# Unread mask matmuls, another split of normalisation and copies, and a third probability buffer in the first attention batch

## The chip, the cores and the metric

The kernel runs on one core of a Trainium2 chip. The metric is the device time of one execution in microseconds (us). TensorE does matrix products, VectorE (DVE) and ScalarE (ACT) elementwise work and reductions, GpSimd (POOL) elementwise work between SBUF tiles, and SyncE (SP) issues almost all DMAs.

## The reference

Attention over 8 batches, 8 heads, 576 tokens, 64 features, followed by a two-layer feed-forward network over all 4608 tokens. Heads 0 to 3 have a plain causal window of 32, heads 4 to 7 a dilated one.

```python
scores = scale * np.matmul(q, k.transpose(0, 1, 3, 2))          # scale = 1/8
mask_plain = (rel >= 0) & (rel < 32)
mask_dil = (rel >= 0) & (rel < 128) & (rel % 4 == 0)
scores = np.where(mask, scores, -1e9); scores -= scores.max(-1)
attn = np.exp(scores); attn /= attn.sum(-1) + 1e-09
x = (attn @ v) with heads side by side                           # 4608 x 512
h = x @ w_in; g = where(h > 0, h, exp(min(h, 0)) - 1)            # 4608 x 2048
out = g @ w_out                                                  # 4608 x 512
```

The weights arrive in a 64-bit format. The kernel converts them to float32 on chip, with one scaling on ScalarE (`magnitude`) and three integer operations on VectorE (`convert`).

## The kernel before, in words

Only the blocks inside the window are computed. Heads go in pairs (`hp` 0 to 3), so one batch has four pairs. A pair has 6 query blocks of 96 rows per head, each against short key pieces, so that its probabilities are 96 partitions by 12 by 64 numbers (`sm`).

The change touches the first batch alone (`first_attention`, generators advanced by a list of steps written out by hand). Every instruction of these steps is kept in program order on its engine. For a pair the steps of before are:

- **S**: two mask matmuls set the score bank to 0 or -1e9, then 72 small score matmuls add the scores (banks `a` and `b`, by turns).
- **M**: VectorE takes the maximum (`nmx`, L356) and subtracts it (L359), ScalarE takes the exponential (L361). For pairs 1 to 3 a tiny GpSimd copy (L119) makes the next weight loads wait for the maximum.
- **P**: VectorE sums (L363), adds 1e-9 (L326) and takes the reciprocal (L327). The multiplication (L328) is VectorE's for pairs 0 and 3, GpSimd's for 1 and 2.
- **T** and **U**: TensorE transposes the probabilities against an identity into a bank (`c` or `a`), and eight copies of the two heads bring them into one of two zeroed buffers `pt` (L381 on VectorE, L383 on ScalarE). T has the transposes and the first head's copies, U the second head's.
- **O**: 12 products of `pt` and values into bank `d` or `b`, then ScalarE copies them into `x` (L314, L317).

Letters A to D are weight conversion (A: ScalarE's scaling; B, C, D: the three VectorE operations on the first tile, the second, and the other two). G0, G1 and G2 are single matmuls of the network's first product, `h<-x,a`, one for each pair's slice of `x`. After the list the code emits the network's first 512 tokens: conversion, `h` products, ELU and second products `o_ps`, with batch 1's attention between them; from there on a scheduler sets the order on each engine by estimated times. Everything later, up to the end at 870.7 us, is a long stream of such products on TensorE.

Buffers: probabilities of pairs 1 to 3, and the inputs of pairs 2 and 3, lie in ring slots that weights will use later.

Of the kernel before, what the change touches and what calls it, by code (L numbers as in the profile page):

```python
# [10 lines left out]
F32 = mybir.dt.float32  # L11
# [5 lines left out]
ALU = mybir.AluOpType  # L17
# [4 lines left out]
DM, DFF = H * D, 2048  # L22
NT = B * S
P = 128
# [50 lines left out]
def body(ctx: ExitStack, tc: tile.TileContext, q, k, v, masks, w_in, w_out, out):  # L75
# [18 lines left out]

    early2 = [wst.tile([P, 2, 4 * DM], F32, name=f"r{NR - NE + i}") for i in range(NE)]
    early = [early2[i // 2][:, i % 2, :] for i in range(2 * NE)]
    for z in pt:
        nc.gpsimd.memset(z, 0.0)

    raw2, raw, full4, full2, full = [None] * (NF // 2), [None] * NF, [None] * (NF // 2), [None] * NF, [None] * 2 * NF  # L100
# [217 lines left out]
                                           in_=flat.rearrange("p (s c i) -> p s c i", c=DIL, i=G // DIL)))  # L318
        return last

    def outputs(b, hp, places, vt, tr, keep=lambda ins: ins):
        products(places, vt, tr)
        return copies(b, hp, places, keep)

    def normalise(eng, sm, sums, keep):
        keep(nc.vector.tensor_scalar(out=sums, in0=sums, scalar1=1e-9, scalar2=None, op0=ALU.add))  # L326
        keep(nc.vector.reciprocal(out=sums, in_=sums))  # L327
        return keep(eng.tensor_tensor(out=sm, in0=sm, in1=sums.unsqueeze(2).broadcast_to([QB, 2 * NU, 2 * G]), op=ALU.mult))  # L328

    def transposed():  # L330
        count[0] += 1
        return pt[count[0] % len(pt)]
# [5 lines left out]
    def first_attention(hp, loaded):  # L338

        dil = hp >= NPAIR // 2  # L340
        qt, kt, vt = loaded
        if hp > 0:
            room, o = (early[0], WINDOW + 2 * S) if hp == 1 else (early[2 * (hp - 2) + 1], 2 * NU * D)
            sm = room[:QB, o:o + 2 * NU * 2 * G].rearrange("p (u j) -> p u j", u=2 * NU)
        else:
            sm = ap.tile([QB, 2 * NU, 2 * G], F32, name="sm", bufs=1)
        mx = ap.tile([QB, 2 * NU], F32, name="nmx", bufs=4)
        sums = ap.tile([QB, 2 * NU], F32, name="sums", bufs=4)
        s_ps = ps_f.tile([P, 2, TC], F32, name="ab"[hp % 2])[:QB, :, :NU * 2 * G]
        for h in range(2):  # L350
            mm(s_ps[:, h, :], ones_sb, mask_sb[:, int(dil), :], start=True, stop=False)
        scores([s_ps[:, h, :] for h in range(2)], qt, kt, False)
        yield
        s4 = s_ps.rearrange("p h (n j) -> p h n j", n=NU)
        mx4 = mx.rearrange("p (h n) -> p h n", h=2)
        inorder(nc.vector.tensor_reduce(out=mx4, in_=s4, op=ALU.max, axis=mybir.AxisListType.X))  # L356
        if hp > 0:
            load_w(hp, mx)
        inorder(nc.vector.tensor_tensor(out=sm.rearrange("p (h n) j -> p h n j", h=2), in0=s4,  # L359
                                        in1=mx4.unsqueeze(3).broadcast_to([QB, 2, NU, 2 * G]), op=ALU.subtract))  # L360
        inorder(nc.scalar.activation(out=sm, in_=sm, func=AF.Exp, scale=0.125))  # L361
        yield
        inorder(nc.vector.tensor_reduce(out=sums, in_=sm, op=ALU.add, axis=mybir.AxisListType.X))  # L363
        last = normalise(nc.vector if hp in (0, NPAIR - 1) else nc.gpsimd, sm, sums, inorder)
        if hp == NPAIR - 1:
            last_step[hp] = last.ins
        yield
        tr = transposed()

        t_ps = (ps_c, ps_f)[hp % 2].tile([P, 2, TC], F32, name="ca"[hp % 2])  # L370
        for n in range(NU):
            for h in range(2):
                o = n % NA * QB
                mm(t_ps[h * 2 * G:(h + 1) * 2 * G, n // NA, o:o + QB], sm[:, h * NU + n, :], ident, start=True, stop=True)
        t4 = t_ps[:, :, :NA * QB].rearrange("p i (n q) -> p i n q", n=NA)
        for h in range(2):
            to = tr[:, h * NU:(h + 1) * NU, :].rearrange("p (i n) q -> p i n q", i=2)
            for c, r, m in ((0, 0, 2), (1, 0, 1), (1, 1, 1), (2, 0, 2)):
                cs, ks, rs = slice(c * G, (c + 1) * G), slice((c + r) * G, (c + r + m) * G), slice((h * 2 + r) * G, (h * 2 + r + m) * G)
                if hp == NPAIR - 1 or (hp, h) == (1, 0):  # L380
                    inorder(nc.vector.tensor_copy(out=to[ks, :, :, cs], in_=t4[rs, :, :, cs]))  # L381
                else:
                    inorder(nc.scalar.copy(out=to[ks, :, :, cs], in_=t4[rs, :, :, cs]))  # L383
            yield
        a_ps = ps_f.tile([P, 2, TC], F32, name="db"[hp % 2])
        yield outputs(0, hp, [(a_ps[:, i, :], i * NA, (i + 1) * NA) for i in range(NU // NA)], vt, tr, inorder)

    def exponential(u, sm, nmx, sums):
        nc.scalar.activation(out=sm[:, u, :], in_=sm[:, u, :], func=AF.Exp, bias=nmx[:, u:u + 1], scale=0.125, accum_out=sums[:, u:u + 1])  # L389
# [558 lines left out]
    its = [first_attention(hp, rooms[hp]) for hp in range(NPAIR)]  # L948


    for what in "S0 S1 M0 M1 S2 P0 M2 T0 U0 S3 P1 P2 A0 M3 T1 U1 O0 T2 U2 P3 B0 O1 T3 U3 O2 G0 G1 O3 G2 A1 C0 D1".split():
        i = int(what[1])
        if what == "G0":
            ps_second.close()
# [2 lines left out]
        if what[0] == "A":  # L957
            inorder(magnitude(i))
        elif what[0] in "BCD":
            last_conversion = convert(i // 2, inorder, {"B": slice(0, DM), "C": slice(DM, 2 * DM), "D": slice(2 * DM, 4 * DM)}[what[0]])  # L960
        elif what[0] == "G":
            next(first)
        else:
            last_copy = next(its[i])
    ready = 2
# [173 lines left out]
```

## Time and profile before

| what | value |
|---|---|
| three runs, median | 873.62 us (872.38 to 873.66) |
| profiled execution: its time, its span | 872.5 us, 870.7 us |
| TensorE busy | 853.7 us (98%) |
| VectorE, ScalarE busy | 555.7 us (64%), 526.9 us (61%) |
| GpSimd busy | 75.0 us (9%) |
| first network product `h<-x,a` starts | 28.02 us |
| granted TensorE clock, mean | 0.996 |

The span runs from the first to the last instruction; 1.8 us of the execution lie outside it. A timeline row gives start, duration from the first start to the last end, engine, line, operation, output and inputs, and a count; in brackets stands how long the engine was idle before, and who ended that. The records of TensorE count two passes for each float32 product, so 12 products appear as x24, and the recorded matmul durations overlap: what one costs in a stream is the distance between starts.

### The profile page before, as it was taken

What the parts mean: (1) busy time and instruction counts of PE and PEld (TensorE: products, weight loads), DVE (VectorE), ACT (ScalarE), POOL (GpSimd) and SP (SyncE); (2) the same over time, 40 slices, a digit from 0 to 9 for tenths busy, and PEclk for the clock granted to TensorE, in tenths of its full rate; (3) what the DMA queues carried; (4) which work ended last, traced back from release to release, by engine and by line L of the source; (5) the groups of instructions that cost most, each with busy time, mean ns of one, the idle gap of its engine ahead of it and who ended that gap; (6) DMA issues with size and microseconds to landing.
All of it is one profiled execution on the core that took longest, in us unless ns stands there. A gap on an engine that the chain in (4) does not pass through costs nothing.

```text
span 870.7 us, 17559 instructions
## 1 busy us (share of the span) xinstructions
PE 853.7 (98%) x6788; PEld 722.5 (83%) x6788; DVE 555.7 (64%) x902; ACT 526.9 (61%) x1031; POOL 75.0 (9%) x112
## 2 busy tenths in 40 slices
PE   6999999999999999999999999999999999999998
PEld 4556878888878889888878898988899988999986
DVE  6899987766685857787765577545476635344431
ACT  3767987756585756667654575654566654555541
POOL 2013311000020200111010020100011100000000
PEclk8999999999999999999999999999999999999999
DMA  9997335134546346867753867662875652776441
GB/s 343 378 381 264 132 123 188 34 132 133 176 160 200 102 151 215 262 221 239 231 173 100 279 200 242 212 184 83 265 226 175 206 164 80 241 209 191 143 153 56
DMA packets 93459, 166.48 MB, mean 191 GB/s; under 512 B 9696, under 2 KB 40768, under 8 KB 93376
## 3 DMA queue, kind: packets, MB, share of 16 engines
q1 hardware_dynamic: 89200, 158.01, 57.0%
q10 hardware_dynamic: 4176, 7.34, 2.3%
q8 instruction: 54, 0.88, 0.4%
q14 instruction: 29, 0.24, 0.1%
HBM read 124.42 MB, written 40.89 MB: 190 GB/s over the span
## 4 chain that ended last, share of the span: by engine, by line
PE 84%; DVE 7%; ACT 4%; DMA 2%; issue 2%; POOL 1%; SPq 0%; ACTq 0%; DVEq 0%; POOLq 0%
PE o_ps L111 41%; PE h L111 34%; PE a_ps L111 8%; DVE a L152 1%; DMA out<-e 1%; POOL pt L435 1%; DVE a L154 1%; DMA r<-combined 1%; DVE nmx L410 1%; ACT sm L389 0%; ACT pt L383 0%; DVE sm L397 0%; PE a L111 0%; DMA kt<-k 0%; DVE a L144 0%
## 5 line engine op out<-in xcount | busy, mean ns | idle before, releaser
L111 PE MATMUL h<-xall,r 128*128 128x384 f32 (+1 forms) x708 | 156.9, 363 | 0.4 <-DVE e L634 0.2
L111 PEld LDWEIGHTS h<-xall,r 128*128 128x128 f32 x708 | 127.7, 188 | 17.2 <-issue 0.8
L111 PE MATMUL o_ps<-a,gh 128*128 128x512 f32 x394 | 129.0, 416 | 0.0
L448 DVE SCALAR_TENSOR_TENSOR a-1_3369<-a-1_3369,a 128x768 f32<-128x768 f32 x64 | 61.0, 953 | 87.9 <-ACT a L448 87.9
L111 PE MATMUL h<-r,r 128*128 128x384 f32 x476 | 108.3, 337 | 0.4 <-DMA r<-combined 0.4
L448 ACT COPY e<-h 128x384 f32<-128x384 f32 x96 | 46.0, 479 | 98.5 <-PE h L111 96.6
L111 PEld LDWEIGHTS o_ps<-a,gh 128*128 128x128 f32 x394 | 73.4, 188 | 21.8 <-issue 9.1
L448 ACT ACTIVATE a<-a-1_3369 128x384 f32<-128x384 f32 (+1 forms) x96 | 60.8, 634 | 50.0 <-DVE a-1_3369 L448 44.0
L111 PEld LDWEIGHTS h<-r,r 128*128 128x128 f32 x476 | 84.4, 188 | 4.0 <-ACT e L448 0.7
L111 PE MATMUL o_ps<-r,gh 128*128 128x512 f32 x242 | 75.4, 393 | 0.0
L111 PE MATMUL o_ps<-a,r 128*128 128x512 f32 x288 | 72.3, 392 | 0.0
L111 PE MATMUL o_ps<-a,gl 128*128 128x512 f32 x173 | 67.7, 391 | 0.0
L448 ACT ACTIVATE a<-a 128x768 f32<-128x768 f32 (+1 forms) x72 | 60.8, 845 | 1.9
L111 PEld LDWEIGHTS o_ps<-a,r 128*128 128x128 f32 x288 | 53.7, 188 | 9.9
L111 PE MATMUL h<-a,r 128*128 128x384 f32 x256 | 60.1, 336 | 0.0
L448 DVE TENSOR_TENSOR a-1_3369<-h,e 128x384 f32<-128x384 f32 x64 | 35.2, 550 | 34.8 <-PE h L111 34.7
L111 PEld LDWEIGHTS o_ps<-r,gh 128*128 128x128 f32 x242 | 44.9, 188 | 8.6
L111 PEld LDWEIGHTS h<-a,r 128*128 128x128 f32 x256 | 46.4, 188 | 4.2
L111 PE MATMUL o_ps<-r,gl 128*128 128x512 f32 x117 | 46.0, 393 | 0.2 <-DVE gl L448 0.2
L435 POOL COPY pt<-sm 32x384 f32<-32x384 f32 x36 | 32.9, 913 | 103.1 <-DVE sm L432 102.1
L111 PE MATMUL o_ps<-a,xall 128*128 128x512 f32 x153 | 39.5, 393 | 0.0
L637 DVE SCALAR_TENSOR_TENSOR e<-h,e 128x512 f32<-128x512 f32 x30 | 20.9, 696 | 27.1 <-ACT e L636 27.1
(219 smaller groups left out, 1553.6 us busy)
## 6 DMA issues: line engine op xcount, KB each, us to landing
r<-combined SPq DMA_DIRECT2D x224, 256.0 KB, 3.6
aside<-a-1_3369 SPq DMA_DIRECT2D x64, 192.0 KB, 3.4
vt<-v SPq DMA_DIRECT2D x30, 384.0 KB, 4.4
kt<-k SPq DMA_DIRECT2D x30, 304.0 KB, 4.9
qt<-q SPq DMA_DIRECT2D x30, 288.0 KB, 4.2
r<-w_in SPq DMA_DIRECT2D x16, 512.0 KB, 7.9
r<-w_out SPq DMA_DIRECT2D x16, 512.0 KB, 8.3
combined<-a SPq DMA_DIRECT2D x20, 256.0 KB, 3.2
```

Of the source, the lines that this page charges most:

```text
L111: return inorder(nc.tensor.matmul(*args, **kw))
L152: keep(nc.vector.scalar_tensor_tensor(out=au, in0=hi, scalar=0x80000000, in1=au, op0=ALU.bitwise_and, op1=ALU.bitwise_or))
L154: return keep(nc.vector.scalar_tensor_tensor(out=au, in0=lo, scalar=29, in1=au, op0=ALU.logical_shift_right, op1=ALU.bitwise_or))
L410: nc.vector.tensor_reduce(out=nmx, in_=sm, op=ALU.max, axis=mybir.AxisListType.X)
L435: last_transpose[b] = (nc.gpsimd.tensor_copy if r else nc.scalar.copy)(out=tr[ks, :, cs], in_=sm[cs, :, rs]).ins
L448: return lambda *args, **kw: inorder(getattr(self.eng, name)(*args, **kw))
L637: v.scalar_tensor_tensor(out=e, in0=h_ps, scalar=0.0, in1=e, op0=ALU.max, op1=ALU.subtract)
```

## The change

A tile `least` holds 1e-9 in every element, and the addition of 1e-9 in the first batch becomes an addition of two tiles. Pair 0's multiplication goes from VectorE to GpSimd, as for pairs 1 and 2; pair 3's stays on VectorE. A third zeroed buffer for probabilities lies in the slot of a later weight tile (`a7`) and serves pair 3. All eight copies of pair 2 are VectorE's; those of pairs 0, 1 and 3 are ScalarE's (before: pair 3's and one head of pair 1 on VectorE, the rest on ScalarE). O is split into the products (O) and the copies into `x` (X). Two new steps, W0 and W1, issue 16 and 7 matmuls of the mask into bank `d`, which nobody reads.

```diff
+    least = const.tile([QB, 2 * NU], F32, name="least")
+    nc.gpsimd.memset(least, 1e-9)
+    third = wst.tile([P, 4, DM], F32, name="a7").rearrange("p t c -> p (t c)")[:, :2 * NU * QB].rearrange("p (u q) -> p u q", u=2 * NU)
-    for z in pt:
+    for z in (*pt, third):
         nc.gpsimd.memset(z, 0.0)
...
+        if least is None:
+            keep(nc.vector.tensor_scalar(out=sums, in0=sums, scalar1=1e-9, scalar2=None, op0=ALU.add))
+        else:
+            keep(nc.vector.tensor_tensor(out=sums, in0=sums, in1=least, op=ALU.add))
...
-        last = normalise(nc.vector if hp in (0, NPAIR - 1) else nc.gpsimd, sm, sums, inorder)
+        last = normalise(nc.vector if hp == NPAIR - 1 else nc.gpsimd, sm, sums, inorder, least)
...
-        tr = transposed()
+        tr = third if hp == NPAIR - 1 else pt[1 - hp % 2]
...
-                if hp == NPAIR - 1 or (hp, h) == (1, 0):
+                if hp == 2:
                     inorder(nc.vector.tensor_copy(out=to[ks, :, :, cs], in_=t4[rs, :, :, cs]))
...
+        products(places, vt, tr)
+        yield
+        yield copies(0, hp, places, inorder)
+
+    def keep_busy(n):
+
+        to = ps_f.tile([P, 2, TC], F32, name="d")
+        for _ in range(n):
+            mm(to[:QB, 0, :NU * 2 * G], ones_sb, mask_sb[:, 0, :], start=True, stop=True)
...
-    for what in "S0 S1 M0 M1 S2 P0 M2 T0 U0 S3 P1 P2 A0 M3 T1 U1 O0 T2 U2 P3 B0 O1 T3 U3 O2 G0 G1 O3 G2 A1 C0 D1".split():
+    for what in "S0 S1 M0 M1 S2 W0 P0 M2 T0 U0 S3 W1 P1 P2 A0 M3 T1 U1 O0 X0 P3 B0 T2 U2 T3 U3 O1 X1 O2 G0 X2 O3 X3 G1 G2 A1 C0 D1".split():
...
+        elif what[0] == "W":
+            keep_busy((16, 7)[i])
```

TensorE from the transposes of pair 1 to the network's first products, before. Banks `a` and `c` receive transposes, `d` and `b` the products with values (`vt`, or for pairs 2 and 3 a part of slots `r_80` and `r_81`), `h_484` the network's product.

```order
L111 MATMUL a<-ident,r_80 64x96 x12
L111 MATMUL d<-pt_79,vt 64x96 x12
L111 MATMUL c<-ident,r_80 64x96 x12
L111 MATMUL b<-pt_78,vt 64x96 x12
L111 MATMUL a<-ident,r_81 64x96 x12
L111 MATMUL d<-pt_79,r_80 64x96 x12
L111 MATMUL h_484<-x_142,a_357 128x512 x2
L111 MATMUL b<-pt_78,r_81 64x96 x12
L111 MATMUL h_484<-x_142,a_357 128x512 x2
```

The same place on TensorE in the change (`a_84` is the third buffer, `h_511` the network's product; the first two rows end the seven matmuls of W1).

```order
L114 LDWEIGHTS masks_sb
L114 MATMUL d<-masks_sb 96x384
L114 MATMUL a<-ident,r_80 64x96 x12
L114 MATMUL d<-pt_79,vt 64x96 x12
L114 MATMUL c<-ident,r_80 64x96 x12
L114 MATMUL a<-ident,r_81 64x96 x12
L114 MATMUL b<-pt_78,vt 64x96 x12
L114 MATMUL d<-pt_79,r_80 64x96 x12
L114 MATMUL h_511<-x_146,a_386 128x512
L114 MATMUL b<-a_84,r_81 64x96 x12
L114 MATMUL h_511<-x_146,a_386 128x512 x3
```

Pair 3's transposes now precede pair 1's products, and pair 3's products stand behind one product of the network instead of two.

VectorE at pair 3's maximum and the conversion B0, before:

```order
L359 TENSOR_TENSOR r_81<-b,nmx 96x768
L381 COPY pt_78<-a 64x6x32
L381 COPY pt_78<-a 32x6x32 x2
L381 COPY pt_78<-a 64x6x32
L363 TENSOR_REDUCE sums<-r_81 96x12
L326 TENSOR_SCALAR sums<-sums 96x12
L327 RECIPROCAL sums<-sums 96x12
L328 TENSOR_TENSOR r_81<-r_81,sums 96x768
L144 TENSOR_SCALAR a_357<-a_357 128x512
L152 SCALAR_TENSOR_TENSOR a_357<-r_137,a_357 128x512
L154 SCALAR_TENSOR_TENSOR a_357<-r_137,a_357 128x512
L381 COPY pt_78<-a 64x6x32
```

The same place on VectorE in the change:

```order
L361 TENSOR_TENSOR r_81<-b,nmx 96x768
L365 TENSOR_REDUCE sums<-r_81 96x12
L328 TENSOR_TENSOR sums<-sums,least 96x12
L329 RECIPROCAL sums<-sums 96x12
L330 TENSOR_TENSOR r_81<-r_81,sums 96x768
L147 TENSOR_SCALAR a_386<-a_386 128x512
L155 SCALAR_TENSOR_TENSOR a_386<-r_141,a_386 128x512
L157 SCALAR_TENSOR_TENSOR a_386<-r_141,a_386 128x512
L383 COPY pt_79<-c 64x6x32
```

The four copies of pair 1 between pair 3's subtraction and its sum are gone, and the eight copies behind the conversion are pair 2's from bank `c` instead of pair 3's from bank `a`. From C0 on the order is the same as before up to one exchange of neighbours; in later stages the scheduler exchanges some neighbours too, and TensorE's order behind this place does not change.

## Rows read from the trace of the kernel before

**Rows 1.** The page: TensorE's busy time, and its granted clock in 40 slices of the span (tenths).

```profile
PE 853.7 (98%) x6788; PEld 722.5 (83%) x6788; DVE 555.7 (64%) x902; ACT 526.9 (61%) x1031; POOL 75.0 (9%) x112
...
PEclk8999999999999999999999999999999999999999
```

**Rows 2.** The waits of TensorE from 31 us to the end: who waited for whom, us in total, times, longest.

```profile
PE h L111 <- ACT h L624: 1.4, 2, 1.2
PE h L111 <- DVE h L193: 1.0, 1, 1.0
```

**Rows 3.** Busy time by stretches of the span, all engines, with the granted clock (PEclk, third from the end), DMA share and GB/s.

```profile
15.00:15.50 0.50, 0.50 (x2) 0.05 (x2) 0.50 (x2) 0.06 (x1) 0.00 (x0) 0.53 1.05 408
...
18.00:21.00 3.00, 2.60 (x32) 2.60 (x34) 2.65 (x5) 2.47 (x5) 1.94 (x3) 0.50 1.03 403
21.50:21.70 0.20, 0.20 (x8) 0.20 (x6) 0.20 (x1) 0.00 (x0) 0.00 (x0) 0.50 0.88 348
...
22.00:28.00 6.00, 4.97 (x104) 4.43 (x98) 5.73 (x13) 5.03 (x16) 0.00 (x0) 1.00 1.02 404
```

**Rows 4.** The timeline of TensorE, first 48 us.

```profile
9.15 0.87 PE L111 MATMUL a<-masks_sb 96*96 96x384 bf16 x2
9.96 1.52 PE L111 MATMUL a<-r 64*32 64x64 f32 x72
13.75 1.21 PE L111 MATMUL c<-ident,sm 96*64 96x96 f32 x24 [2.27 <-DVE sm L328]
14.89 0.78 PE L111 MATMUL b<-masks_sb 96*96 96x384 bf16 x2
15.60 1.52 PE L111 MATMUL b<-r 64*32 64x64 f32 x72
18.40 2.19 PE L111 MATMUL a<-ident,r 96*64 96x96 f32 x24 [1.28 <-POOL r L328]
20.37 1.88 PE L111 MATMUL d<-pt,vt 128*64 128x96 f32 x24
...
24.73 1.21 PE L111 MATMUL a<-ident,r 96*64 96x96 f32 x24
...
26.89 1.20 PE L111 MATMUL d<-pt,r 128*64 128x96 f32 x22 [0.82 <-ACT pt L383]
28.02 1.99 PE L111 MATMUL h<-x,a 128*128 128x512 f32 x4
29.94 1.21 PE L111 MATMUL b<-pt,r 128*64 128x96 f32 x24
...
36.44 0.97 PE L111 MATMUL a_ps<-kt,qt 64*32 64x64 f32 x72
...
44.48 2.11 PE L111 MATMUL h<-xall,h 128*128 128x512 f32 x8
47.63 1.19 PE L111 MATMUL h<-xall,h 128*128 128x512 f32 x4 [1.03 <-DVE h L193]
```

**Rows 5.** The timeline of TensorE much later, two matmuls of 384 columns in a stream.

```profile
602.45 0.33 PE L111 MATMUL h<-r,r 128*128 128x384 f32 x1
602.62 0.34 PE L111 MATMUL h<-a,r 128*128 128x384 f32 x1
```

**Rows 6.** The timeline of VectorE.

```profile
12.34 0.22 DVE L327 RECIPROCAL sums<-sums 96x12 f32<-96x12 f32 x1
...
16.30 0.17 DVE L326 TENSOR_SCALAR sums<-sums 96x12 f32<-96x12 f32 x1
...
17.57 0.80 DVE L326 TENSOR_SCALAR sums<-sums 96x12 f32<-96x12 f32 x1
...
22.18 0.95 DVE L363 TENSOR_REDUCE sums<-r 96x12 f32<-96x768 f32 x1
...
26.29 2.99 DVE L381 COPY pt<-a 64x192 f32<-64x192 f32 x8
...
32.96 0.69 DVE L144 TENSOR_SCALAR a<-a 128x1024 uint32<-128x1024 uint32 x1 [1.77 <-ACT a L136]
...
46.89 0.68 DVE L193 TENSOR_TENSOR h<-a,h 128x512 fp32r<-128x512 f32 x1
...
75.78 2.96 DVE L154 SCALAR_TENSOR_TENSOR a<-r,a 128x2048 uint32<-128x2048 uint32 x1
```

**Rows 7.** VectorE's groups of instructions by line and shape, 0 to 130 us: count, busy us, mean ns.

```profile
L152 DVE SCALAR_TENSOR_TENSOR a<-r,a 128x2048 uint32<-128x2048 uint32 x6 | 13.7, 2285 | 0.1
```

**Rows 8.** The timeline of ScalarE.

```profile
16.19 2.64 ACT L383 COPY pt<-c 64x192 f32<-64x192 f32 x8
18.85 1.15 ACT L136 ACTIVATE a<-r 128x1024 f32<-128x1024 f32 x1
20.46 0.84 ACT L361 ACTIVATE r<-r 96x768 f32<-96x768 f32 x1 [0.46 <-DVE r L359]
...
31.20 0.70 ACT L314 COPY x<-b 128x288 f32<-128x288 f32 x2 [2.36 <-PE b L111]
```

**Rows 9.** The timeline of GpSimd.

```profile
0.73 2.05 POOL L98 MEMSET pt<- 128x1152 f32 x2 [0.29 <-POOLq L1130]
...
16.88 1.47 POOL L328 TENSOR_TENSOR r<-r,sums 96x768 f32<-96x768 f32 x1 [2.21 <-ACT pt L383]
...
74.90 1.70 POOL L328 TENSOR_TENSOR sm<-sm,sums 96x768 f32<-96x768 f32 x1 [13.03 <-DVE sums L327]
```

More of the change, by code (lines that the diff above doesn't have):

```diff
@@ L319, in copies, with normalise @@
         return last
[L321 to L326, printed above, removed]
+    def normalise(eng, sm, sums, keep, least=None):
+        if least is None:
+            keep(nc.vector.tensor_scalar(out=sums, in0=sums, scalar1=1e-9, scalar2=None, op0=ALU.add))
+        else:
+            keep(nc.vector.tensor_tensor(out=sums, in0=sums, in1=least, op=ALU.add))
         keep(nc.vector.reciprocal(out=sums, in_=sums))
@@ L385, in first_attention @@
         a_ps = ps_f.tile([P, 2, TC], F32, name="db"[hp % 2])
-        yield outputs(0, hp, [(a_ps[:, i, :], i * NA, (i + 1) * NA) for i in range(NU // NA)], vt, tr, inorder)
+        places = [(a_ps[:, i, :], i * NA, (i + 1) * NA) for i in range(NU // NA)]
+        products(places, vt, tr)
[5 more added lines that the diff above has]
+            mm(to[:QB, 0, :NU * 2 * G], ones_sb, mask_sb[:, 0, :], start=True, stop=True)
     def exponential(u, sm, nmx, sums):
```

## The prediction

> **What bounds the kernel now.** I read the page first. TensorE is busy for 98% of the span and its clock is at full in all slices but the first [rows 1], so an edit of the first 30 us counts only by what it leaves of TensorE's later stream. Next I read the waits of TensorE from 31 us to the end. There are few, and the longest one inside the reach of the first batch is 1.03 us, for VectorE's split of a weight [rows 2], at 47.63 [rows 4]. So the end of the kernel moves as that restart at 47.63 moves. It comes from the later of two chains. TensorE would have been ready at 44.48 + 2.11 = 46.6 [rows 4]. VectorE ended the split at 46.89 + 0.68 = 47.57 [rows 6]. VectorE's chain there runs back to 32.96, where it waited 1.77 us for ScalarE's scaling [rows 6]; that stood behind ScalarE's copies of pair 3 at 31.20, which waited 2.36 us for pair 3's products [rows 8], which TensorE began at 29.94 [rows 4].
>
> So two times matter: when pair 2's products begin (26.89), since TensorE has no pause behind them until 46.6, and when pair 3's begin (29.94), since VectorE's chain hangs on them. In before, pair 3's products stood behind two network products of 0.86 each (four records in a stream between 28.02 and 29.74, then 0.2 before the next group) [rows 4].
>
> **TensorE's clock.** I read it from durations where the slices of the page are too wide. 72 score matmuls take 1.52 at 9.96 and 0.97 at 36.44 [rows 4]: they ran at the low level (1.2 GHz) until 11.48, with work and no pause from 9.15 on. The transposes at 13.75 take 1.21, as at 24.73 [rows 4], the high level (2.4 GHz), so the clock rose in the pause between. It then fell: 0.53 in the half microsecond from 15.00, 0.50 from 18 to 21 and still at 21.5, and 1.00 from 22 on [rows 3]. What went before the fall is a pause of 2.27 us [rows 4]. In the low stretch the same transposes took 2.19 and the products 1.88 instead of 1.20 [rows 4].
>
> **The change part by part.**
>
> *W0, 16 mask matmuls.* Not shown in before. In a stream at the high level one costs 602.62 - 602.45 = 0.17 [rows 5], at the low level (9.96 - 9.15) / 2 = 0.40 [rows 4]. They start near 11.4. All at the high level they end at 14.1; if the clock rises only at 13.75 they end near 15.5. I take 14.3, about one at the low level, because the clock had to rise after work that was already done at 11.48.
>
> *Pair 0's multiplication to GpSimd.* The reciprocal ends at 12.56 [rows 6]. GpSimd takes 1.47, and began at 16.88 some 0.15 behind the reciprocal that follows the addition of 16.30 [rows 6, 9]: 14.2, against 13.55 on VectorE (an instruction of this size takes 0.95 there, as at 22.18 [rows 6]). W0 covers that. The transposes move from 13.75 to 14.3, 0.55 later. VectorE is free some 0.9 earlier, so pair 2's maximum and subtraction, and the two sums, move up by as much.
>
> *The larger memsets.* The third buffer adds one of the two memsets' 1.03 each [rows 9] before the identity is made at about 4 us; first use is at 14.3. Nothing.
>
> *Pair 3's scores and W1.* Transposes 1.14 (13.75 to 14.89), two mask matmuls 0.34, scores 0.97: 16.75, at the high level. VectorE comes free for pair 3's maximum at about 17.0 and ends the subtraction at 18.9. Seven mask matmuls end near 17.8. Pair 1's multiplication on GpSimd runs from 15.9 to 17.4, so pair 1's transposes end at 19.0 instead of 20.6 [rows 4].
>
> *ScalarE.* Pair 0's transposes end at 14.3 + 1.21 = 15.5. Copies 2.66, up to the scaling's start (16.19 to 18.85), scaling 1.15 [rows 8]: pair 3's exponential starts at 19.4, behind ScalarE and not behind the subtraction (18.9), and ends at 20.25; before it started at 20.46 [rows 8]. Then pair 1's eight copies, 2.64, end at 22.9, so pair 3's transposes into the same bank run from about 22.95 to 24.2. ScalarE's copies of pair 3 (0.7 for pair 0's `x`, then 2.64 from 24.2) end near 26.9 and pair 1's `x` copies at 27.6, which frees bank `b`.
>
> *VectorE to pair 2's copies.* From pair 3's sum (22.18) to the end of the eight copies behind B0 (26.29 + 2.99 = 29.28) VectorE took 7.10 with no pause [rows 6]. The same row of instructions, with pair 2's copies for pair 3's, now starts at 20.26 and ends at 27.36. The copies that left VectorE saved their 1.44 and the exponential's earlier start saved the rest.
>
> *Pair 2's products.* Their copies are VectorE's last work now. They restart at 27.40 instead of 26.89: 0.51 later. That is the price of the split; the pause that stands before it is new, from about 25.4.
>
> *Pair 3's products.* 27.40 + 1.13 (26.89 to 28.02) + 0.86 + 0.2 = 29.59 instead of 29.94: 0.35 earlier, because one network product now stands behind them. Pair 3's buffer (26.9) and bank (27.6) are ready.
>
> *The end.* ScalarE's scaling, VectorE's conversion and the split come 0.35 earlier: 47.22. TensorE would be ready at 46.6 + 0.51 = 47.1. The restart is VectorE's still: 47.28, gain 0.35. With s for pair 2's lateness, the gain is 0.86 - s. Behind 47.63 the order on TensorE is unchanged and everything before it shifts together; the exchanges of neighbours by the scheduler lie where TensorE doesn't wait, and I count them at nothing, plus or minus 0.3. The weight loads that wait for pair 2's inputs start 0.5 later and have some 3 us until ScalarE's scaling of them.
>
> The sum: 872.5 - 0.35 = 872.15 for the profiled execution, which is 1.1 below the median; the median comes to 873.62 - 0.35 = 873.3.
>
> *The addition of 1e-9 with `least`.* In before the scalar form took 0.80 instead of 0.17 while GpSimd multiplied from 16.88 to 18.35: it ended with GpSimd [rows 6, 9]. The form with two tiles is not shown beside GpSimd at this size. Bounds: 0.17, and until GpSimd ends. Pair 2's addition falls at 16.6, inside pair 1's multiplication (15.9 to 17.4). A larger instruction with two SBUF inputs took 2.96 beside GpSimd's 74.90 to 76.60, and 2.285 on average [rows 6, 7, 9]: 0.68 lost in an overlap of 0.82, so it crept but ran. I take 0.25. Waiting to 17.4 moves the subtraction's end from 18.9 to 19.4, level with ScalarE, and costs at most 0.1 at the end.
>
> The Trainium skill speaks against this edit: "GPSIMD Engine Reference", section "Key points", says that GpSimd shares its SBUF interfaces with VectorE and contends with instructions in a two-port mode or with two SBUF inputs. By that rule the new form suffers too; the trace agrees for the large form. The sum by the rule is 873.4, by the row of 0.17 it is 873.3.
>
> **The rivals.**
>
> *The clock falls again in the new pause (20%).* For it: a pause of 2.27 came before the fall at 15.0, and now TensorE stands still from about 25.4 to 27.4, after another pause of 1.5 before pair 3's transposes. Against: the pause of 0.82 at 26.89 did nothing. The price: the low stretch in before lasted from 15.0 to 21.7 [rows 3]; at half rate it costs TensorE 3.3, and half as long 1.7. TensorE would then be ready at 47.1 + 1.7 to 3.3 = 48.8 to 50.4, which is 1.2 to 2.8 behind 47.63: 874.8 to 876.4, middle 875.6. It decides as soon as TensorE loses more than 0.5.
>
> *The whole low stretch is on the path (18%).* Full clock saves TensorE 0.37 on the masks, 0.55 on pair 3's scores, 0.98 on pair 1's transposes and 0.68 on the products [rows 4]: 2.6, and 871.0. For it: VectorE and ScalarE waited for each of these in turn. Against: I find ScalarE's queue (copies, scaling) setting the exponential, not TensorE.
>
> *W0 is too long (9%).* If the clock rises only at 13.75, pair 0's transposes start at 15.5, the exponential at 20.6, s becomes 1.7 and the kernel loses 0.85: 874.5.
>
> *The unread matmuls don't hold the clock (5%).* It falls at 15.0 as before; W1 then costs 7 x 0.40 = 2.8 before pair 1's transposes, which end near 22.3, and pair 1's copies at 25.0 hold back pair 3's transposes and products: about 29.9, nothing gained, 873.7.
>
> **How the numbers follow.** The forecast has 48%: 873.3, with its own range 872.3 to 874.4 (the three runs lie within 1.3, s between 0.2 and 1.2). About 0.2% (1.75 us) is what a measurement can tell from no change, so faster means under 871.9 and slower over 875.4. Faster: nearly all of the second rival and little else, 0.18. Slower: two thirds of the first rival and the tails of the third, 0.16. The rest is 0.66. The range reaches to the second rival's value and to the middle of the first: 871.0 to 875.7.
>
> **What would show it.** Clock 1.00 from 14 to 22, transposes of pairs 0 and 1 at 1.2 both. Pair 3's exponential starting straight behind the scaling near 19.4. Pair 2's copies ending on VectorE near 27.4 and its products right behind. Pair 3's products near 29.6. The restart for the split near 47.3, with a wait of about 0.2. The addition with `least` inside GpSimd's multiplication well under 0.8. I am wrong if the first network products run at half rate, if pair 2's products start before 26.5 or after 28.2, or if TensorE shows new waits behind 48.

## The result, and the profile after

The change made the kernel slower by 1%: 882.08 us (median of 4 runs, 879.59 to 883.73) against 873.0 (4 runs, 871.46 to 873.66) in the same comparison. The ratio is 1.0104, 95% interval 1.0074 to 1.0134. The profiled execution took 883.02 us, its span 881.2. The forecast was 873.3, its range went up to 875.7.

The page of the changed kernel, busy time of the engines and the granted clock in 40 slices, as in [rows 1]:

```profile
PE 860.6 (98%) x6811; PEld 725.5 (82%) x6811; DVE 552.6 (63%) x897; ACT 528.3 (60%) x1035; POOL 78.8 (9%) x115
...
PEclk8899999999999999999999999999999999999999
```

TensorE is busy 6.9 us longer with 23 more matmuls, and a second slice falls below full clock. Both point at the first 45 us. Its timeline there, to be laid beside [rows 4]:

```profile
10.93 1.52 PE L114 MATMUL a<-r 64*32 64x64 f32 x72
14.74 3.95 PE L114 MATMUL d<-masks_sb 96*96 96x384 bf16 x16 [2.29 <-issue]
18.62 2.19 PE L114 MATMUL c<-ident,sm 96*64 96x96 f32 x24
...
22.99 1.35 PE L114 MATMUL d<-masks_sb 96*96 96x384 bf16 x7
24.27 1.21 PE L114 MATMUL a<-ident,r 96*64 96x96 f32 x24
...
28.62 1.21 PE L114 MATMUL a<-ident,r 96*64 96x96 f32 x24 [1.15 <-ACT pt L385]
...
31.79 0.35 PE L114 MATMUL d<-pt,r 128*64 128x96 f32 x2 [0.97 <-DVE pt L383]
33.10 2.03 PE L114 MATMUL d<-pt,r 128*64 128x96 f32 x22 [0.96 <-DVE pt L383]
35.06 1.93 PE L114 MATMUL h<-x,a 128*128 128x512 f32 x2
36.92 1.21 PE L114 MATMUL b<-a,r 128*64 128x96 f32 x24
...
54.62 1.19 PE L114 MATMUL h<-xall,h 128*128 128x512 f32 x4 [0.47 <-DVE h L196]
```

W0 (the 16 matmuls) doesn't stand in the pause behind pair 2's scores. It begins 2.29 us after them, with nothing to wait for that the profile shows, and takes 3.9 us up to pair 0's transposes, which start at 18.62 instead of 13.75. ("issue" stands where the profile shows nothing that the engine waited for.) The restart for the split weight comes at 54.62 instead of 47.63: 7.0 us are lost by then. The granted clock by stretches (third number from the end of a row), to be laid beside [rows 3]:

```profile
14.00:16.00 2.00, 1.26 (x8) 0.99 (x9) 1.97 (x3) 0.56 (x1) 1.36 (x2) 1.00 1.03 412
...
18.00:22.00 4.00, 4.00 (x58) 2.63 (x62) 0.59 (x2) 1.05 (x4) 1.81 (x2) 0.50 1.04 414
...
24.00:33.00 9.00, 6.02 (x125) 5.21 (x122) 7.77 (x17) 7.70 (x22) 0.18 (x1) 1.00 0.67 230
...
35.00:36.50 1.50, 1.50 (x3) 0.50 (x2) 0.00 (x0) 0.70 (x2) 0.00 (x0) 0.50 0.37 55
```

There are two low stretches (1.2 GHz) now: one as in before, behind the first pause, and a new one from about 33 to 36.7, behind the pauses before pair 3's transposes and pair 2's products. VectorE and GpSimd:

```profile
17.57 0.80 DVE L328 TENSOR_TENSOR sums<-sums,least 96x12 f32<-96x12 f32 x1
...
23.15 0.95 DVE L358 TENSOR_REDUCE nmx<-b 96x12 f32<-96x768 f32 x1 [4.53 <-PE b L114]
...
30.10 2.94 DVE L383 COPY pt<-c 64x192 f32<-64x192 f32 x8
```

```profile
16.87 1.47 POOL L330 TENSOR_TENSOR r<-r,sums 96x768 f32<-96x768 f32 x1 [1.51 <-DVE sums L329]
```

The addition of two tiles took 0.80 and ended with GpSimd's multiplication (18.34), as the scalar form had [rows 6, 9]. VectorE waited 4.53 us for pair 3's scores, and pair 2's copies ended at 33.04. Behind 31 us the waits of TensorE (as [rows 2]) are more, but short:

```profile
PE h L114 <- issue: 2.0, 2, 1.5
PE d L114 <- DVE pt L383: 1.9, 2, 1.0
PE h L114 <- ACT h L635: 1.9, 3, 1.0
PE h L114 <- DVE h L196: 0.5, 1, 0.5
```

The span is 10.5 us longer, and 7.0 were lost by 54.62. So 3.5 came later, where I had counted nothing.

### The profile page after: what moved, and what is told of

It is laid out like the page before. It is cut to its first block, busy times and chain, and to the rows that moved or that the text cites. A ratio compares the mean times of both kernels' runs of the same rounds, so it can differ in the third digit from the quotient of the medians.

```text
span 881.2 us, 17611 instructions
## 1 busy us (share of the span) xinstructions
PE 860.6 (98%) x6811; PEld 725.5 (82%) x6811; DVE 552.6 (63%) x897; ACT 528.3 (60%) x1035; POOL 78.8 (9%) x115
## 4 chain that ended last, share of the span: by engine, by line
PE 80%; ACT 7%; DVE 5%; DMA 4%; issue 3%; POOL 1%; SPq 0%; ACTq 0%; DVEq 0%; POOLq 0%
PE o_ps L114 39%; PE h L114 32%; PE a_ps L114 7%; ACT sm L400 1%; DMA kt<-k 1%; DMA whole<-a 1%; DMA r<-w_out 1%; PE d L114 1%; POOL pt L446 1%; DVE a L155 1%; ACT a L139 1%; PE b L114 1%; DMA out<-h 1%; ACT a L459 0%; DVE a L157 0%
## 5 line engine op out<-in xcount | busy, mean ns | idle before, releaser
L114 PEld LDWEIGHTS o_ps<-a,gl 128*128 128x128 f32 x173 | 32.5, 188 | 6.8
```

What stands on the lines that cost most here:

```text
L114: return inorder(nc.tensor.matmul(*args, **kw))
```

## The experiments

Two numbers are read from each profiled execution: the shift of the restart for the split weight against 47.63 [rows 4], and the span against 870.7. Their difference is what was lost or won behind 48 us. Both come from one execution, the median from all. "Later order" says whether the rows of ScalarE and VectorE behind 48 us stand in the order of before.

| version | median us | ratio, 95% | shift at restart | at the end | behind | later order |
|---|---|---|---|---|---|---|
| the change | 882.08 | 1.0104 (1.0074 to 1.0134) | +7.0 | +10.5 | +3.5 | other |
| change without W0, W1 | 877.86 | 1.0059 (1.0039 to 1.0080) | +2.8 | +5.5 | +2.7 | other |
| before with W0, W1 | 879.82 | 1.0076 (1.0049 to 1.0103) | +5.4 | +7.6 | +2.2 | other |
| change, W0 ahead of pair 2's scores | 876.98, one run | | +3.0 | +4.5 | +1.5 | other |
| change, W0 of 2, no W1 | 878.96, one run | | +3.6 | +6.5 | +2.9 | other |
| no W, pauses filled later | 877.06 | 1.0044 (1.0029 to 1.0059) | +1.3 | +4.4 | +3.1 | other |
| no W, old split of copies | 875.73 | 1.0029 (1.0019 to 1.0038) | -1.9 | +0.3 | +2.2 | other |
| the same, pair 0 on VectorE | 872.79 | 0.9999 (0.9989 to 1.0008) | +0.4 | +0.8 | +0.4 | as before, six rows of VectorE exchanged |
| no W, pair 0 on VectorE | 874.88 | 1.0034 (1.0018 to 1.0050) | +1.8 | +1.3 | -0.5 | as before, but for a few rows |
| before, third buffer | 872.65 | 1.0004 (0.9994 to 1.0014) | +0.3 | +0.3 | 0 | as before |
| before, W0 of 2 | 872.89 | 1.0000 (0.9988 to 1.0012) | +0.5 | -0.8 | -1.3 | as before |
| before, W0 of 4 | 874.80 | 1.0016 (1.0006 to 1.0027) | +0.6 | +3.0 | +2.4 | other |
| before, pair 3 behind one product | 874.34 | 1.0012 (1.0001 to 1.0022) | +0.2 | +3.2 | +3.0 | other |
| before, one exchange at 142 us | 874.46 | 1.0019 (1.0009 to 1.0029) | +0.4 | +2.7 | +2.3 | other behind 142 us |
| pair 0 on VectorE, pair 3 filled | 875.11 | 1.0028 (1.0015 to 1.0040) | 0 | +2.6 | +2.6 | other |

**The unread matmuls.** First the change without them, and then before with them alone (16 and 7, as in the change). The list of steps in the one and the other:

```diff
-S2 W0 P0 M2 T0 U0 S3 W1 P1
+S2 P0 M2 T0 U0 S3 P1
```

```diff
-S2 P0 M2 T0 U0 S3 P1
+S2 W0 P0 M2 T0 U0 S3 W1 P1
```

Without: 

> The change without W0 and W1. Theory 1 (TensorE stands still behind pair 2's scores because its next instructions are not there yet: a 16 KB transfer of the instruction queue begins as the pause begins; so W0 runs behind the pause, on the path): the pause stays near 2.3 us, pair 0's transposes start right behind it or behind GpSimd's multiplication, near 14 to 14.8 and not at 18.6, the first network product starts between 27.5 and 30 instead of 35.1, and 5 to 8 us of the 9 are gone: 873.5 to 877. Rival (the other split of copies and normalisation is what costs): the first network product still starts after 32 and the time stays over 879. Rival (the two low stretches of the clock are the loss, whatever stands in the pause): both low stretches remain, and no more than 2 us come back.

Alone: 

> The kernel before with W0 and W1 alone. Theory 1: W0 starts behind a pause of about 2.3 us, takes 3 to 4 us, and moves pair 0's transposes to 17.5 to 18.7 from 13.75; the time is 878 to 882, most of the 9 us. Rival (the split of the copies is what costs): under 876. Rival (W0 fills the pause): transposes at 14.2 to 15.5 and 872 to 875.

Both put the unread matmuls on the path, with different sizes. Taking them out brings the restart forward by 4.2 us and the ratio down by 0.0045; that is less than the 5 to 8 us expected, and the first network product, at 30.92, was later than the 30 expected, so other parts of the change cost time too. Adding them to before puts the restart back by 5.4 and the ratio up by 0.0076. There the pause was 2.56 us, and all of W0 ran at the low level and took longer than the 3 to 4 us expected:

```profile
13.89 5.36 PE L111 MATMUL d<-masks_sb 96*96 96x384 bf16 x16 [2.56 <-issue]
19.18 2.19 PE L111 MATMUL c<-ident,sm 96*64 96x96 f32 x24
```

Then W0 in another place, and W0 of two matmuls:

```diff
-S2 W0 P0
+W0 S2 P0
```

```diff
-            keep_busy((16, 7)[i])
+            keep_busy((2, 0)[i])
```

Early: 

> The change with W0 moved ahead of pair 2's scores, so that 32 more instructions stand ahead of their end. Theory 1: the pause of about 2.3 us sits at the same number of instructions from the start, so now inside pair 2's scores or at the end of W0, not behind the scores; behind the scores pair 0's transposes start with less than 1 us of pause. Rival (the pause waits for something that pair 0 needs): the pause stays behind pair 2's scores.

Two: 

> The change with two matmuls in W0 and none in W1. Theory 1: TensorE stands still for 2.2 to 2.4 us although W0's first matmul waits for nothing, then the two matmuls take 0.4 to 0.8, then pair 0's transposes, at 14.2 to 15.5. Rival (the pause is data's): the two matmuls run straight behind pair 2's scores, with under 0.2 of pause.

Two matmuls began 2.71 us after the scores, where sixteen had begun 2.29 after them. With W0 ahead of the scores the pause went into the scores:

```profile
12.44 0.80 PE L114 MATMUL a<-r 64*32 64x64 f32 x56
13.65 0.41 PE L114 MATMUL a<-r 64*32 64x64 f32 x16 [0.41 <-issue]
14.27 1.21 PE L114 MATMUL c<-ident,sm 96*64 96x96 f32 x24 [0.20 <-POOL sm L330]
```

It cut them 16 matmuls before their end, and 16 matmuls had been put ahead of them. So the pause belongs to a place in TensorE's stream of instructions, not to data. In all sixteen traces, that of before too, it stands behind TensorE's 222nd matmul (three times 2 mask and 72 score matmuls; with W0 ahead of the scores 16 of the 222 are W0's), and in the six that put unread matmuls or scores behind that place these began at 13.5 to 14.7. That TensorE waits there for its own instructions fits this, and the DMA view shows one packet of the instruction queue just before (in the change from 12 to 14 us, beside 228 packets of data):

```profile
q8 instruction: 1, 0.02, 2.9%
```

No row names the wait itself, but the traces hold more for this cause. Behind 11 us they have 19 pauses of TensorE over 0.2 us that are put down to issue. Each of them ends 1.25 to 1.54 us after a 16 KB packet of that queue has ended, and such packets are rare (54 in the 870 us of before). Ahead of these pauses stand 449, 705, 5057, 7105, 8897 or 10945 recorded instructions of TensorE, numbers that lie whole multiples of 256 apart. No run varied the loading of instructions alone, so the cause is inferred; the place and the packet are shown.

With W0 ahead of the scores the clock was at full from 10 to 30 us in every stretch read, and the restart came no sooner for it than without W0 (+3.0 against +2.8). This doesn't price the clock by itself. Without W0 VectorE waited 1.18 us for pair 3's scores, at the low level; with the early W0 that wait is gone, but VectorE waits 1.52 us for pair 2's scores, which now stand behind 16 matmuls:

```profile
18.86 0.95 DVE L358 TENSOR_REDUCE nmx<-b 96x12 f32<-96x768 f32 x1 [1.18 <-PE b L114]
```

```profile
14.11 0.95 DVE L358 TENSOR_REDUCE nmx<-a 96x12 f32<-96x768 f32 x1 [1.52 <-PE a L114]
```

So held at this price the clock of the first 22 us gained nothing; what it is worth alone stays open.

**The pauses of the new split.** In the version without W0 and W1, on TensorE:

```profile
24.33 1.21 PE L114 MATMUL a<-ident,r 96*64 96x96 f32 x24 [2.40 <-ACT pt L385]
25.37 1.88 PE L114 MATMUL b<-pt,vt 128*64 128x96 f32 x24
...
28.81 2.18 PE L114 MATMUL d<-pt,r 128*64 128x96 f32 x22 [0.75 <-DVE pt L383]
30.92 1.88 PE L114 MATMUL h<-x,a 128*128 128x512 f32 x2
```

Pair 1's eight copies are all ScalarE's now, and pair 3's transposes wait 2.40 us for them. Behind that pause the clock fell, and was at 0.50 from 26 to 32. Is the fall the cost, or the wait? Unread matmuls were put into these later pauses:

```diff
-B0 T2 U2 T3 U3 O1 X1 O2 G0
+B0 T2 U2 W0 T3 U3 O1 X1 W1 O2 G0
...
-            keep_busy((16, 7)[i])
+            keep_busy((12, 6)[i], "bd"[i])
```

> The change without W0 and W1, with 12 unread mask matmuls put before pair 3's transposes (bank b) and 6 before pair 2's products (bank d), where the change's other parts leave TensorE new pauses of 2.4 and some 1 us. Theory (the fall of TensorE's clock behind these pauses is the cost at the end of the first batch, not the pauses): no low stretch from 25.6 to 32.5, first network product at 30.0 or earlier instead of 30.92, restart for the split weight at 48.5 to 49.3 instead of 50.45, so 1.2 to 2.0 us under the version without these matmuls: about 876. Rival (the waits for the copies are the cost themselves, the clock only follows): first network product at 30.5 or later and the restart at 50.2 to 50.6, about 877.9. A third way: the added instructions lengthen TensorE's own stream and the clock falls elsewhere; then the restart is later than 50.6.

The clock from 26 to 32 us without and with them:

```profile
26.00:32.00 6.00, 5.00 (x42) 3.63 (x38) 4.45 (x11) 3.55 (x11) 0.00 (x0) 0.50 0.46 180
```

```profile
26.00:32.00 6.00, 5.63 (x80) 3.93 (x78) 4.65 (x12) 3.89 (x12) 0.00 (x0) 1.00 0.46 178
```

The restart came at 48.89 instead of 50.45, as the theory had it: in these two executions the fall costs 1.6 us. The medians, 877.06 and 877.86, differ by 0.8, and their intervals overlap. The other 1.3 of the shift stood with the clock held; I put them down to the waits, which no run shows alone. Then the old split:

```diff
-                if hp == 2:
+                if hp == NPAIR - 1 or (hp, h) == (1, 0):
```

> The change without W0 and W1, and with the copies shared out as before (pair 3 and one head of pair 1 on VectorE, the rest on ScalarE); the third buffer, the addition of two tiles, pair 0's multiplication on GpSimd and the new order of pairs 2 and 3 stay. Theory (the new split of the copies makes the pauses before pair 3's transposes and pair 2's products): the pause of 2.4 us before pair 3's transposes under 1, pair 2's products begin before 27.3, the first network product at 29.0 or earlier, the restart for the split weight at 48.0 to 49.0, and 875 to 876.5 in all. Rival (pair 0's multiplication on GpSimd and the low clock under pairs 0 to 3 set it): first network product at 30 or later as without this edit, 877 to 878.

```profile
23.43 1.21 PE L114 MATMUL a<-ident,r 96*64 96x96 f32 x24 [1.58 <-DVE r L330]
...
26.69 1.13 PE L114 MATMUL h<-x,a 128*128 128x512 f32 x2
...
45.69 1.19 PE L114 MATMUL h<-xall,h 128*128 128x512 f32 x4 [0.49 <-DVE h L196]
```

The pause before pair 3's transposes was 1.58 us instead of the under 1 expected, now a wait for VectorE's multiplication. In this execution the first batch even gained 1.9 us on before, more than expected. But the profiled execution, 872.77, was the fastest of ten, and the median is 3 us above it. What the others did in the first batch no trace shows.

**Pair 0's multiplication.** It went back to VectorE, with the old split (there with the scalar addition) and with the new one (there `least` stays).

```diff
-        last = normalise(nc.vector if hp == NPAIR - 1 else nc.gpsimd, sm, sums, inorder, least)
+        last = normalise(nc.vector if hp in (0, NPAIR - 1) else nc.gpsimd, sm, sums, inorder)
```

Old split: 

> The version with the old split of the copies, with pair 0's multiplication back on VectorE and the addition of 1e-9 back in its scalar form. Of the change there stay the third buffer, pair 3's transposes before pair 1's products, the split of products and copies, and pair 3's products behind one network product instead of two. The later order on ScalarE is that of before in every row, on VectorE it has six rows exchanged. Theory (the later order, not the first batch, took back what the old split gained): the gain at 48 us is 1 to 2.5 us as with GpSimd, it is kept to the end within 0.7, 871 to 872.5, faster than before. Rival (any shift in the first batch is taken back by later transfers): the gain at 48 us is gone by 280 us, 873 or more. Another (pair 0's multiplication on GpSimd made the gain): nothing gained at 48 us.

New split: 

> The change without W0 and W1 and with pair 0's multiplication on VectorE; the change's split of the copies stays, and nearly all of the later order is that of before. Theory (the split costs about 2.8 us at 48 us, and the exchanged later order cost another 3 in the version with GpSimd): shift of +2 to +3.5 at 48 us and no more than 1 on top of it, 875.5 to 877. Rival (GpSimd's multiplication for pair 0 made the split late): shift at 48 us under 1.2. Another rival (the late loss comes with any shift): 878 or more.

Before with the third buffer alone:

> The kernel before with the third buffer alone (its list of steps and copies as before, pair 3 in the third buffer); the later order is that of before in every row. Theory (the gain of the version with the old split comes from the new order of steps, the buffer alone frees nothing that anyone waits for): shift at 48 us between -0.4 and +0.3, 873. Rival (the buffer lets pair 3's copies start earlier and makes the gain): -1 or more at 48 us and 872.

The two splits and the two engines make a table of two by two results, medians and ratios:

| | old split | new split |
|---|---|---|
| pair 0 on VectorE | 872.79, 0.9999 | 874.88, 1.0034 |
| pair 0 on GpSimd | 875.73, 1.0029 | 877.86, 1.0059 |

The split costs 0.0035 or 0.0030, some 3 us. The move to GpSimd costs 0.0030 or 0.0025. With the new split the traces say where: 1.0 us up to the restart and 3.2 behind it (+2.7 against -0.5). With the old split they don't, since the execution with GpSimd was the fastest of its ten and ended before the one with VectorE. The buffer alone is worth nothing, as expected. With the new split the shift (+1.8) and the median came out a little under the 2 to 3.5 and 875.5 to 877 expected. The expectation that the gain at the restart would stay in the first of these missed: +0.4 instead of -1.9, and the median stayed at that of before. Here the pause before pair 3's transposes was followed by a low stretch:

```profile
24.46 1.83 PE L112 MATMUL a<-ident,r 96*64 96x96 f32 x24 [1.70 <-DVE r L328]
26.02 2.19 PE L112 MATMUL b<-pt,vt 128*64 128x96 f32 x24
```

**The later order.** In before, 2 and 4 unread matmuls, which differ little in the first batch; the scheduler gives the first the later order of before in every row, and the second another. The edit of the first (the second has 4 for the 2):

```diff
+S2 W0 P0
...
+            keep_busy((2, 0)[i])
```

Two: 

> The kernel before with 2 unread mask matmuls behind pair 2's scores; the later order of instructions on VectorE, ScalarE and SyncE is the same as before. Theory (the late loss of 2 to 4 us comes from the scheduler's exchanged order): the first batch shifts by 0.2 to 0.9, and what it shifts at 48 us it shifts at the end, within 0.5: 873.0 to 874.0. Rival (the late loss comes from any shift in the first batch, by the timing of later transfers or of instruction loading): growth of 1 us or more between 48 us and the end.

Four: 

> The kernel before with 4 unread mask matmuls behind pair 2's scores, two more than in the version above; here the scheduler exchanges many instructions of the later stages on VectorE and ScalarE. Theory (the exchanged order costs): the shift at 48 us is 0.3 to 1.6, and 1 to 3 us are added behind it, 875 to 877. Rival (the order makes no difference): the shift at the end is that at 48 us within 0.5, under 874.5.

The restart shifts by 0.5 and 0.6, the end by -0.8 and +3.0, and the ratios are 1.0000 and 1.0016. That is the way the theory said, with both medians just under the range expected and the first version drifting by 1.3 where 0.5 was allowed; its profiled execution was the fastest of its ten. But in the second 1.3 of the 2.4 us behind the restart are a pause at 628.37, which ends 1.43 us after a packet of the instruction queue:

```profile
628.37 0.96 PE L111 MATMUL h<-r,r 128*128 128x384 f32 x4 [1.32 <-issue]
```

So this pair doesn't separate the order from the loading of instructions. Then before with one step of the list moved:

```diff
-O2 G0 G1 O3 G2
+O2 G0 O3 G1 G2
```

> The kernel before with one change in the list of steps: pair 3's products stand behind one network product instead of two, the change's one step that was to bring time forward. Theory, two parts. First, the step is worth up to 0.86 us where no pause is added: first network product at 28.3 to 28.8 as in the other versions of before, restart for the split weight 0.5 to 0.9 earlier against it than the 19.6 us of before. Second, the later order costs: with this list the scheduler puts ScalarE's activation of the probabilities ahead of the copy of the network's first product near 142 us, as in the two versions that lost 1.8 to 3.8 us there. So TensorE waits 1 to 2 us at that place, the gain at 48 us is gone by 160 us, and in all 872.7 to 874.5. Rival (the exchanged order is harmless, the earlier losses came of the shift itself): no wait over 0.5 us near 142, gain kept, 871.5 to 872.3.

The step brought 0.8 us: the restart stands 18.8 us behind the first network product instead of 19.6 (that product came at 29.04, later than expected, behind a low stretch that lasted beyond 22). And the order took it back. The shift was -0.3 at 116 us, +1.2 at 143 and +2.3 at 149, with a wait of 1.28 us at 144.22 for the copy that stands behind the activation. In this version a shift and an order still came together, so last the exchange by itself: a copy of the network's first product on ScalarE is bound behind the activation of batch 2's first probabilities. Up to there all rows stand as in before.

```diff
-            a.copy(out=h, in_=h_ps)
+            with tc.issue_after(active[2, 0]) if (c, f) == (1, 1) else nullcontext():
+                a.copy(out=h, in_=h_ps)
```

> The kernel before with one copy of the network's first product bound behind the activation of batch 2's probabilities on ScalarE, near 142 us, as the scheduler had put them in the versions that lost time there; up to that place every instruction stands as before, behind it the scheduler's order differs. Theory (the exchanged order is a cost of its own): shift before 140 us within 0.4 of nothing; TensorE waits 1 to 2 us for that copy near 142 and is 1.5 to 3 us late at 160; in all 874 to 876.5. Rival (the late loss comes of the shift in the first batch): no wait over 0.5 us there, 872 to 873.5.

ScalarE and TensorE at that place in before:

```profile
140.51 0.59 ACT L624 COPY h<-h 128x512 f32<-128x512 f32 x1 [0.69 <-PE h L111]
...
143.13 0.85 ACT L418 ACTIVATE sm<-sm 96x768 f32<-96x768 f32 x1 [0.89 <-DVE sm L417]
```

```profile
142.81 0.39 PE L111 MATMUL o_ps<-r,gl 128*128 128x512 f32 x1
143.03 2.20 PE L111 MATMUL h<-xall,r 128*128 128x512 f32 x9
```

and with the exchange:

```profile
143.35 0.84 ACT L419 ACTIVATE sm<-sm 96x768 f32<-96x768 f32 x1 [3.31 <-DVE sm L418]
144.10 0.56 ACT L627 COPY h<-h 128x512 f32<-128x512 f32 x1
```

```profile
143.02 0.39 PE L112 MATMUL o_ps<-r,gl 128*128 128x512 f32 x1
144.72 1.65 PE L112 MATMUL h<-xall,r 128*128 128x512 f32 x6 [1.31 <-ACT h L627]
```

The activation waits 3.31 us for VectorE. The copy, which in before ran at 140.51, stands behind it, and TensorE's next product needs the bank that it frees: a wait of 1.31 us, and 0.2 us of lateness at 137 became 1.7 there and 2.7 at the end. By the medians this order costs 1.9 us without a shift in the first batch. In the profiled execution 1.5 of the 2.7 us came at this place; the rest came behind it, where many other rows are exchanged too. The rival falls for this version.

The change itself does not have that wait: there the copy, at 147.01, still runs ahead of the activation, at 149.61. TensorE waits 1.3 to 1.8 us for this copy, between 142 and 149 us, in seven versions: the change without W0 and W1, with W0 of two, with the pauses filled later and with the old split; before with pair 3 behind one product and with the one exchange; and the last one below. In the first and the last of these seven the clock also fell behind the wait (0.50 from 149 to 151.5 and from 146.5 to 149.5). In the change TensorE waits 0.99 us for a later copy of ScalarE, near 156, as the two versions with pair 0 on VectorE and the old order do (0.98 and 0.99). And it pauses three times with nothing to wait for: 0.52 us at 285.96, 0.44 at 396.84 and 1.46 at 500.79:

```profile
500.79 1.20 PE L114 MATMUL h<-xall,r 128*128 128x384 f32 x6 [1.46 <-issue]
```

They end 1.29 to 1.49 us after a packet of the instruction queue, as the pause ahead of W0 does. So 2.4 us of waits of this kind stand in the change's 3.5 us. Before has no such pause over 0.2 us; whether the exchanged rows or the shift brought them is not shown.

At last the pause before pair 3's transposes was filled in the version with pair 0 on VectorE:

```diff
-B0 T2 U2 T3
+B0 T2 U2 W0 T3
...
+            keep_busy(6, "b", 128)
```

> The version with pair 0's multiplication on VectorE and the old copies, with 6 unread mask matmuls of 128 columns (about 0.4 us) put before pair 3's transposes, where TensorE stood still for 1.70 us and its clock fell. Theory (the fall of the clock behind that pause took 1.5 us of the first batch's gain): no low stretch from 24.5 to 28.5, first network product at 26.7 to 28.0 instead of 29.23, shift at 48 us of -1.3 to -2.2. The later order is exchanged again, so 1.5 to 3 us come back behind 140 us: 872.5 to 874.5 in all. Rival (the clock's fall is harmless, VectorE sets that stretch): first network product at 28.8 or later and -0.7 or less at 48 us. A third way (the pause's rest, 1.3 us, is still enough for a fall): as before, first product at 29 or later and the low stretch is there.

The pause shrank to 0.68 and the clock held from 24 to 29 us. But the first product came at 28.68, not before 28.0, and nothing was gained at the restart: in this execution the first low stretch lasted to about 23, beyond the 22 of before [rows 3], and pair 2's transposes were 0.9 us later than in before by then. The median, 875.11, lies 2.3 us above the version without the six matmuls and above the range expected; the wait for the exchanged copy, 1.78 us at 144.68, and the fall of the clock behind it came with the new order. So this run shows that the clock held where the pause was filled, and leaves open what that is worth here. No version was measurably faster than before.

## Why the prediction was wrong

**W0 covers the pause, pair 0's transposes at 14.3** (failed, about 4 us). I read the 2.27 us before 13.75 [rows 4] as a wait for VectorE only, since that is whom the row names. There was a second wait under it, at the same place and nearly as long, which no semaphore ends. Two versions without W0 show it: VectorE's multiplication ended at 13.65 (pair 0 on VectorE, old split) and 13.58 (one exchange), and the transposes began at 14.14 and 14.47; in before it took 0.20 from the one to the other. The 16 matmuls came behind this wait and stood on the path. Without W0 the transposes began at 14.33, when GpSimd had multiplied, close to the 14.2 that I had for GpSimd. "Full clock from 14 to 22" fell with this step: the clock was 0.56 from 16 to 18 and 0.50 from 18 to 22, although W0 ran from 14.74 on. The rivals "W0 is too long" (9%) and "the unread matmuls don't hold the clock" (5%) had what happened, but were priced at 0.85 us and at nothing gained.

**s = 0.51, pair 2's products at 27.40** (failed, 1.4 us). Without W0 and W1 they restarted at 28.81. The part from pair 3's sum to the end of the copies took 7.04 us there (21.71 to 28.75) for my 7.10. Its start was wrong: pair 3's exponential began at 20.83 and not at 19.4, still behind VectorE's subtraction and not behind ScalarE's scaling. The subtraction in turn stood behind the 1.18 us that VectorE waited for pair 3's scores, which ran at the low level. So my ground against the second rival, that ScalarE's queue and not TensorE sets the exponential, was wrong. The room that this was to make for the split wasn't there.

**The clock falls again** (a rival at 20%) is what happened in the new pauses: I had named both, and priced the fall at 1.7 to 3.3 us of TensorE; filling the pauses gave back 1.6 at the restart, between two single executions. The two pauses should have made this the likeliest case.

**Everything behind 47.63 shifts together, the scheduler's exchanges nothing, plus or minus 0.3** (failed, 3.5 us). In the change itself 2.4 us of waits are the three pauses behind packets of the instruction queue, for which my sum had no term, and 0.99 is the wait near 156, which versions with the order of before have too. So its trace does not show that the exchanges took the 3.5 us; what brought the pauses stays open. In seven other versions an exchange does cost time: I had looked only at whether TensorE waited there in before, and the question is what the earlier one of the new pair waits for. Versions with the later order of before, in all or nearly all rows, drifted by -1.3 to +0.4 behind 48 us, the others by +1.5 to +3.5, for either reason.

**`least`, 0.25 us** (failed, small). It took 0.80, 0.63 more than alone, and ended with GpSimd. The Trainium skill's rule ("GPSIMD Engine Reference", "Key points", contention with instructions of two SBUF inputs) agrees with the trace here, and for so small an instruction the delay lasted until GpSimd was through. The scalar form had taken 0.80 at the same place [rows 6], so the new form neither helped nor cost. My choice of the row nearest to the lower end was the wrong one.

**Right:** pair 3's products behind one network product instead of two. In the version with that step alone they began 1.05 us behind the first product instead of 1.92 [rows 4], 0.87 for my 0.86. The larger memsets and the third buffer cost nothing. The restart hangs on VectorE's split (a wait of 0.47), as forecast.

Taken out one after the other, the parts are by the ratios: unread matmuls 0.0045, pair 0 on GpSimd with the order that came with it 0.0025, split of copies 0.0035, and the rest nothing. That this comes to 0.0105 for the 1.0104 follows from the way of reckoning, since the last version stands at 0.9999. It is no test: put into before alone, the unread matmuls cost 0.0076, so the parts don't simply add.

## What to carry to other kernels

A pause that a row puts down to one engine can have a second cause under it; put two matmuls into it before sixteen, and see when they start. Where a pause is put down to issue, look at when the last packet of the instruction queue ended. Count a change at the head of a scheduled program together with the order that the scheduler gives the rest: look at what the instruction that moved ahead waits for, and who stands behind it. When work is shared out anew between engines, price the pause that it leaves on TensorE by the clock as well as by its length.

## What the hardware showed that I had not expected

- TensorE paused 2.3 to 3.1 us (2.29, 2.56, 2.71, 2.87, 3.05) behind pair 2's scores without a semaphore to wait for, and the pause moved with the count of instructions ahead of it. This and 14 more such pauses, up to 628 us into the kernel, ended 1.25 to 1.54 us after a 16 KB packet of the instruction queue, at places that lie multiples of 256 of TensorE's recorded instructions apart.
- The clock of one list differs between executions: pair 1's transposes took 1.21 at 18.50 in one and 2.19 at 19.09 in another, with the same instructions ahead. A pause of 1.58 us was not followed by a fall, one of 1.70 at the same place was. The Trainium skill ("TensorE: Matmul & The Clock Gate", Part 1) also calls the length of the slow start run-variable; here the first network product came at 26.69 without the fall and at 29.23 with it, in two versions that also differ in pair 0's multiplication and the form of the addition.
- An addition of 12 elements per partition took 0.80 us instead of 0.17 beside GpSimd's multiplication, in both of its forms, while the sum just before it (16.64 to 17.53, one input of 768 elements) took 0.89 beside the same multiplication, no longer than another alone (0.95 at 26.00).
